# Small marker loads behind the big loads of a fused attention-plus-GLU decode kernel

## The chip, the cores and the metric

The kernel runs on one core of one Trainium2 chip. The metric is device time in microseconds (us). The profile is one profiled execution; its span, from the first to the last instruction that the profile shows, is a little shorter than the device time, which also holds what lies around it.

## What is computed

One decode step for two batch rows: a layer norm of x, then attention with 32 heads over the last 2048 positions of the caches, and beside it a gated linear unit without a nonlinearity. All is float32.

```python
xn = _layernorm(x)
q = (xn @ wq)                                     # 2 rows, 32 heads of 128
scores = einsum("bhqd,bhkd->bhqk", q, k[..., -2048:, :]) * 128 ** -0.5
a = einsum("bhqk,bhkd->bhqd", softmax(scores), v[..., -2048:, :]) @ wo
h = (xn @ w_gate) * (xn @ w_up)                   # 1376 wide
return x + a + h @ w_down
```

Nearly all bytes are the caches: K and V of 32 heads for two rows. Every byte is used once.

## The kernel before

The host lays out all weights and caches in one long array, `stream`, in the order in which the kernel uses them. `blocks()` (L45) gives that order as a list of loads; each load is a list of fields (a head's K, 4096 floats wide in each of 128 partitions, a head's V, a slice of a weight). The first load goes to a tile of its own, `first`, 542 floats wide. All others go to step tiles: `steps` (L128) is a pool with three buffers of 128 partitions by STEP = 13824 floats (L39), that is 55296 bytes in each partition. Most loads fill a step tile; those at the end of the stream are smaller, and several share a tile.

`pump()` (L143) issues loads from SP until three step tiles are held; `done()` (L166) counts a field as used up, and when the last field of a tile is used, it frees the tile and calls `pump()` again, so that the next load is issued then. The load into a freed buffer waits on SP until VectorE and TensorE have finished with the buffer. All loads go out on SP's DMA queue, in order. Two small DMAs stand behind the fourth load on the same queue: `x_nat` (L182), 16 rows of 128 floats, and `carry` (L185), 9 rows of 9 floats. The result goes out at L531.

For each head VectorE multiplies K with the projected query in place (`products`, L277) and sums over the head dimension (`sums`, L285); GpSimd and ScalarE make the softmax; TensorE weighs V, and projects queries, outputs and the gated unit. One such step over a head's K occupies VectorE for two instructions over 4096 floats.

`InOrder` (L83) keeps each engine's instructions in the order in which the program lists them, and records all of them under one line, L98; in the profile, operations are told apart by their tiles. SP executes in order as well: an instruction that waits holds back all behind it.

Tiles of the pool `const` (L127) lie one behind the other in each partition in the order in which they are made, and the step tiles lie behind them. A DMA counts as landed when a semaphore says so; the small tile's dependencies are tracked tile by tile, so that two DMAs that write the same tile are ordered by a wait.

Of the kernel before, what the change touches and what calls it, by code (L numbers as in the profile page):

```python
# [8 lines left out]
F32 = mybir.dt.float32  # L9
# [18 lines left out]
RB = 8  # L28
M = RB * (B - 1) + 1
# [84 lines left out]
def kernel(  # L114
# [8 lines left out]
    pe, dve, act, sp = (InOrder(tc, e) for e in (nc.tensor, nc.vector, nc.scalar, nc.sync))  # L123
# [3 lines left out]
    const = ctx.enter_context(tc.tile_pool(name="const", bufs=1))  # L127
# [8 lines left out]
        todo.append((key, fields, at))  # L136
        at += P * sum(w for _, _, w in fields)
    tiles, used, left, got = {}, {}, {}, {}
    held = 0
    for key, fields, _ in todo:  # L140
        left[key] = left.get(key, 0) + len(fields)

    def pump():  # L143
        nonlocal held
        while todo:
            key, fields, at = todo[0]
            if key not in tiles:
                if key[0] == "f":
                    n = sum(w for _, _, w in fields)
                    tiles[key] = const.tile([P, n], F32, name="first")  # L150
                elif held == BUFS:
                    return
                else:
                    held += 1
                    tiles[key] = steps.tile([P, STEP], F32, name="step")
                used[key] = 0
            todo.pop(0)
            c0 = used[key]
            for kind, i, w in fields:
                got[kind, i] = (tiles[key][:, used[key] : used[key] + w], key)  # L160
                used[key] += w
            c1 = used[key]
            src = stream[at : at + P * (c1 - c0)].rearrange("(p i) -> p i", p=P)
            sp.dma_start(tiles[key][:, c0:c1], src)

    def done(kind, i):  # L166
        nonlocal held
        _, key = got.pop((kind, i))
        left[key] -= 1
        if left[key] == 0 and key[0] != "f":  # L170
            del tiles[key]
            held -= 1
            pump()

    pump()
    xT = got["x", 0][0].rearrange("p (b c) -> p b c", b=B)
    pick = got["pick", 0][0].rearrange("p (r s b) -> p r s b", s=2, b=B)
# [447 lines left out]
```

## Time and profile before

| What | Value |
|---|---|
| Time, median of 3 runs | 377.29 us (377.18 to 377.37) |
| Profiled execution, span | 375.7 us |
| Read from HBM in that span | 159.47 MB |
| Mean DMA rate over the span | 425 GB/s |
| Matmuls, TensorE | 1100 |
| Loads into step tiles | 28 |

How to read the profile: PE is TensorE (PEld its weight loads), DVE VectorE, ACT ScalarE, POOL GpSimd, SP the engine whose queue issues the DMAs; SPq, DVEq are the engines' instruction queues. Rows of grouped instructions read: line, engine, operation, written tile <- read tiles, count. DMA rows give the size of one in KB (1024 bytes) and the time from its issue to its landing. "DMA share" is the mean busy share of the 16 DMA engines; a packet is counted where it starts, so that a short stretch can exceed 1. A queue row reads: packets, MB, and the time that the packets took as a share of 16 engines' time.

### The profile page before, as it was taken

The numbers are of one execution on the slowest core, as the hardware profiler recorded it, in microseconds if no ns is written. First come the engines' busy times: TensorE is split into PE (matmuls) and PEld (weight loads), VectorE is DVE, ScalarE is ACT, GpSimd is POOL, SyncE is SP. The second block draws the span as 40 slices with busy tenths as digits, with TensorE's granted clock in tenths as the row PEclk, the third lists the DMA queues.
The fourth block names the chain that finished last, engine by engine and source line by source line (L and its number), as shares of the span: only waits on it lengthen the run. The fifth ranks groups of instructions, "written<-read, shape, count | busy, mean of one in ns | idle before, by whom it ended". The sixth has DMA issues, their size and how long they took to land.

```text
span 375.7 us, 2891 instructions
## 1 busy us (share of the span) xinstructions
PE 256.5 (68%) x1100; PEld 88.1 (23%) x1100; DVE 294.6 (78%) x147; ACT 58.7 (16%) x259; POOL 25.3 (7%) x78
## 2 busy tenths in 40 slices
PE   3396696986548487864848676485867639637996
PEld 3241122331112122211222211121212213021334
DVE  3299691998599499769949976994996799599960
ACT  1021001122020211201112020111202011121131
POOL 1001000000000000100000100000000000000010
PEclk9796988899696966859686786976669887556999
DMA  8999999899999999999999999999999999999995
GB/s 327 463 436 454 408 426 471 383 465 432 414 465 394 459 424 424 461 400 453 418 437 449 412 447 424 432 442 430 436 436 424 437 434 436 436 425 424 419 421 226
DMA packets 4382, 159.70 MB, mean 425 GB/s; under 512 B 514, under 2 KB 658, under 8 KB 1042
## 3 DMA queue, kind: packets, MB, share of 16 engines
q1 hardware_dynamic: 4370, 159.54, 98.5%
q8 instruction: 8, 0.13, 0.1%
q14 instruction: 4, 0.03, 0.0%
HBM read 159.47 MB, written 0.07 MB: 425 GB/s over the span
## 4 chain that ended last, share of the span: by engine, by line
DMA 62%; DVE 29%; PE 7%; ACT 1%; issue 0%; SPq 0%; DVEq 0%
DMA step<-in_stream_dram 62%; DVE s L98 14%; DVE step L98 14%; PE o_ps L98 3%; PE q L98 2%; PE acc L98 2%; PE tr L98 1%; DVE m L98 0%; ACT o_sb L98 0%; ACT oT L98 0%; SPq L98 0%; DVE rec L98 0%; DVE o_out L98 0%; DVEq L98 0%
## 5 line engine op out<-in xcount | busy, mean ns | idle before, releaser
L98 DVE TENSOR_TENSOR step<-step,q 128x4096 f32<-128x4096 f32 x31 | 136.6, 4408 | 53.3 <-DMA step<-in_stream_dram 53.3
L98 PE MATMUL q<-step,xnb 128*128 128x512 f32 (+1 forms) x128 | 92.7, 874 | 75.5 <-DMA step<-in_stream_dram 75.5
L98 DVE TENSOR_REDUCE s<-step 128x32 f32<-128x4096 f32 x32 | 141.4, 4419 | 1.1
L98 PE MATMUL o_ps<-step,p 128*16 128x512 f32 (+1 forms) x512 | 69.7, 682 | 10.3 <-DMA step<-in_stream_dram 10.3
L98 PEld LDWEIGHTS q<-step,xnb 128*128 128x128 f32 x128 | 32.2, 275 | 128.9 <-DMA step<-in_stream_dram 79.1
L98 PE MATMUL acc<-step,oT 128*9 128x512 f32 (+1 forms) x88 | 35.2, 554 | 9.3 <-ACT oT L98 8.1
L98 PE MATMUL tr<-first,o_sb 128*128 128x2 f32 (+2 forms) x198 | 27.6, 258 | 15.3 <-ACT o_sb L98 12.8
L98 ACT COPY o_sb<-o_ps 128x512 f32<-128x512 f32 (+1 forms) x24 | 13.8, 576 | 143.1 <-PE o_ps L98 143.1
L98 PEld LDWEIGHTS tr<-first,o_sb 128*128 128x128 f32 x198 | 25.5, 196 | 37.3 <-ACT o_sb L98 32.6
L295 POOL PARTITION_ALL_REDUCE mm<-m x32 | 11.3, 354 | 283.4 <-DVE rec L98 178.9
L98 PEld LDWEIGHTS o_ps<-step,p 128*16 128x16 f32 x512 | 13.5, 106 | 70.4 <-issue 55.2
L98 ACT ACTIVATE nm<-mm 128x2 f32<-128x2 f32 x32 | 6.5, 203 | 129.5 <-POOL mm L295 129.5
L98 ACT ACTIVATE p<-s,nm 128x16 f32<-128x16 f32 x64 | 19.2, 300 | 1.0
L98 ACT ACTIVATE oT<-tr,rec 128x1 f32<-128x1 f32 x64 | 12.2, 260 | 28.3 <-PE tr L98 28.3
L311 POOL PARTITION_ALL_REDUCE sum<-rs x32 | 12.7, 398 | 54.8 <-ACT p L98 54.8
L98 PE MATMUL o_ps<-step,xn 128*2 128x512 f32 (+1 forms) x48 | 12.9, 593 | 0.0
L98 ACT ACTIVATION_READ_ACCUMULATOR p<-s,nm 128x1 f32 x64 | 12.0, 187 | 0.0
L98 DVE TENSOR_TENSOR step<-step,tr 128x4096 f32<-128x4096 f32 x1 | 4.4, 4421 | 9.3 <-DMA step<-in_stream_dram 9.3
L98 PEld LDWEIGHTS acc<-step,oT 128*9 128x9 f32 x88 | 4.3, 91 | 19.5 <-ACT oT L98 13.1
L98 PE MATMUL q<-xnb,mean_w 128*128 128x512 f32 (+1 forms) x18 | 8.5, 563 | 0.0
L98 PE MATMUL acc<-step,hT 128*9 128x128 f32 (+2 forms) x58 | 7.9, 357 | 0.0
L98 DVE TENSOR_REDUCE m<-s 128x2 f32<-128x32 f32 x32 | 5.9, 186 | 1.1
(43 smaller groups left out, 36.5 us busy)
## 6 DMA issues: line engine op xcount, KB each, us to landing
step<-in_stream_dram SPq DMA_DIRECT2D x16, 6912.0 KB, 33.7
step<-in_stream_dram SPq DMA_DIRECT2D x2, 6400.0 KB, 32.6
step<-in_stream_dram SPq DMA_DIRECT2D x1, 6720.0 KB, 45.6
step<-in_stream_dram SPq DMA_DIRECT2D x1, 6656.0 KB, 28.9
step<-in_stream_dram SPq DMA_DIRECT2D x1, 5376.0 KB, 15.4
step<-in_stream_dram SPq DMA_DIRECT2D x1, 4864.0 KB, 30.1
step<-in_stream_dram SPq DMA_DIRECT2D x2, 2304.0 KB, 17.2
step<-in_stream_dram SPq DMA_DIRECT2D x1, 2048.0 KB, 15.9
```

The lines of the kernel that those rows point to most:

```text
L98: made = call(*args, **kwargs)
L295: nc.gpsimd.partition_all_reduce(mm, m, P, bass_isa.ReduceOp.max)
L311: nc.gpsimd.partition_all_reduce(sum_t[h], rs, P, bass_isa.ReduceOp.add)
```

## The change

A tile `marks`, 16 partitions of 40 floats (160 bytes in each partition), is made before all others of `const`. `pump()` counts its loads. Behind the sixth to the twentieth load, counted with `first` as number one, it issues one more DMA on SP: k = 1 for the sixth, up to 15 for the twentieth; k rows of 8 + 2k floats each, from the array `x_rows` into `marks`. The fourteenth load (k = 9 = M) has none. Nothing reads `marks`. The computing instructions of the other engines and their order stay the same.

```diff
-    held = 0
+    held = n_loads = 0
+    marks = const.tile([2 * RB, 5 * RB], F32, name="marks")
...
     def pump():
-        nonlocal held
+        nonlocal held, n_loads
...
             sp.dma_start(tiles[key][:, c0:c1], src)
+            n_loads += 1
+            k = n_loads - 5
+            if 0 < k < 2 * RB and k != M:
+                sp.dma_start(marks[:k, : 8 + 2 * k], x_rows[:k, : 8 + 2 * k])
```

## The prediction

> **What bounds the kernel now.** I read the page from the top (busy shares, the DMA line, the chain of waits), then the 50-us windows, then the rows of SP's queue. In the page below, DMA is busy nearly the whole span and the chain that ended last is mostly one kind of wait, a load of the stream:
>
> ```profile
> span 375.7 us, 2891 instructions
> PE 256.5 (68%) x1100; PEld 88.1 (23%) x1100; DVE 294.6 (78%) x147; ACT 58.7 (16%) x259; POOL 25.3 (7%) x78
> ...
> q1 hardware_dynamic: 4370, 159.54, 98.5%
> ...
> DMA 62%; DVE 29%; PE 7%; ACT 1%; issue 0%; SPq 0%; DVEq 0%
> ```
>
> The reader is to see that no engine is near its limit (VectorE, the busiest, has 22% idle) while SP's DMA queue, q1, fills 98.5% of the 16 DMA engines' time. The VectorE pieces of the chain are not a bound of their own: they are the time until a buffer is free, and meanwhile earlier loads still stream, as a window from the middle shows (last two columns: DMA share, GB/s):
>
> ```profile
> 200.00:250.00 50.00, 33.96 (x128) 10.58 (x124) 44.38 (x21) 7.77 (x36) 3.76 (x10) 0.75 1.01 435
> ```
>
> So the time is bytes over about 435 GB/s plus start and end. Anything added to this queue counts in full only if it takes DMA-engine time, or delays an issue until the queue runs dry. I priced both.
>
> **What the change adds.** One tile of 160 bytes per partition, and 14 small DMAs on SP: k from 1 to 15 without 9, k rows each, one behind each big load concerned; k rows because the sum 1+...+15 less 9 is 111 rows. Nothing is removed, and the order of the computing engines' work is the same. The built program shows one wait more: each small DMA writes the tile that the one before wrote, so SP holds it until that one has landed, and the next big load stands behind it.
>
> *DMA-engine time.* The kernel already has such a DMA: `carry`, 9 rows of 36 bytes, behind `x_nat`, 16 rows of 512 bytes, behind a 6720 KB load. Windows on the DMA packets, each on a stretch so short that it holds one packet or a few, give the time of a packet as share x 16 engines x stretch:
>
> ```profile
> DMA packets 1, 0.00 MB, mean 18 GB/s; under 512 B 1, under 2 KB 1, under 8 KB 1
> q1 hardware_dynamic: 1, 0.00, 34.4%
> ...
> DMA packets 1, 0.00 MB, mean 0 GB/s; under 512 B 1, under 2 KB 1, under 8 KB 1
> q1 hardware_dynamic: 1, 0.00, 5.6%
> ...
> q1 hardware_dynamic: 7, 0.00, 12.6%
> ```
>
> The first stretch is 2 ns (46.740 to 46.742 us) and holds one `carry` row: 0.344 x 16 x 2 = 11 ns. The second is 10 ns and holds one semaphore write of 4 bytes: 0.056 x 16 x 10 = 9 ns. The third is 50 ns where x_nat and carry pass: 7 packets in 0.126 x 16 x 50 = 101 ns, 14 ns each. A row of the small loads has 40 to 152 bytes, between carry's 36 and x_nat's 512, so 14 ns is a fair price, and 14 + 9 = 23 ns for row and semaphore. If k rows go to k engines, the busiest engine serves all 14: 14 x 23 = 0.32 us; the mean engine 111 / 16 x 23 ns = 0.16 us. The last load waits for the slowest engine, so between 0 (that engine has slack) and 0.32 us; I take 0.2. The upper bound is by landings:
>
> ```profile
> step<-in_stream_dram SPq DMA_DIRECT2D x1, 6720.0 KB, 45.6
> x_nat<-in_x_rows_dram SPq DMA_DIRECT2D x1, 8.0 KB, 45.3
> ...
> 1.15 1.37 SPq L98 DMA_DIRECT2D step<-in_stream_dram  x3
> 2.56 0.55 SPq L98 DMA_DIRECT2D x_nat<-in_x_rows_dram  x1
> ...
> out_dram<-o_out SPq DMA_DIRECT2D x1, 64.0 KB, 1.5
> ```
>
> The third big load was issued about 2.1 us into the span (three in 1.37 us) and landed at 47.7; x_nat at 2.56 + 45.3 = 47.9. Were this 0.2 us time in which nothing else moved, 14 of them would be 2.8 us: the far end. It should not be, since a completion can trail while the next packets run.
>
> [...]
>
> *The held issues.* SP's rows and the landings of the same loads, each issue looked at by itself:
>
> ```profile
> 73.14 0.33 SPq L98 DMA_DIRECT2D step<-in_stream_dram  x1
> step<-in_stream_dram SPq DMA_DIRECT2D x1, 6912.0 KB, 24.7
> ...
> 83.19 0.33 SPq L98 DMA_DIRECT2D step<-in_stream_dram  x1
> step<-in_stream_dram SPq DMA_DIRECT2D x1, 6912.0 KB, 31.0
> ...
> 92.26 0.33 SPq L98 DMA_DIRECT2D step<-in_stream_dram  x1
> step<-in_stream_dram SPq DMA_DIRECT2D x1, 6912.0 KB, 38.3
> ...
> 126.47 0.33 SPq L98 DMA_DIRECT2D step<-in_stream_dram  x1
> step<-in_stream_dram SPq DMA_DIRECT2D x1, 6912.0 KB, 36.6
> ```
>
> These loads land at 97.8, 114.2, 130.6 and 163.1, so one takes 16.3 us. The small DMA issued behind the load of 83.19 waits for the small one behind the load of 73.14, which lies in the queue behind that load: 97.8 and a little. The load of 92.26 stands behind it on SP and is held to about 99 (6 us late). Its data follow on those of the load landing at 114.2, so it is still 15 us early. The same recurs at every second load, the one issued more than one load ahead now: the load of 126.47 is held until the one landing at 130.6 has landed, 5 us, and 15 us remain. The loads between are issued after that point anyway. Behind the held load on SP there is only its own small DMA; no engine waits for SP itself, and VectorE and TensorE wait for landings, which do not move. Price: 0. Without this cover it would be 5 or 6 us at some six loads, about 33 us. The small DMA's own issue, some 0.55 us as for x_nat, is hidden in the same 15 us.
>
> *The shift by 160 bytes.* The small tile is allocated first, so every later tile moves. In the built program the three step tiles begin at multiples of 2048 bytes in their partition, afterwards 32 bytes past a multiple of 64. What a row there costs no trace of before shows; the nearest rows are the `first` load, 2168-byte rows to a tile that begins 128 bytes past a multiple of 256, from a source whose rows lie 2168 bytes apart, against 2048-byte rows of the last load, well placed:
>
> ```profile
> q1 hardware_dynamic: 78, 0.17, 72.2%
> ...
> q1 hardware_dynamic: 1, 0.00, 52.5%
> ...
> L98 SPq DMA_DIRECT2D step<-in_stream_dram x28: 327/328/432, 1.1 to 353.5; - x28
> ```
>
> The first stretch is 0.6 us: 0.722 x 16 x 600 / 78 = 89 ns a row; the second 10 ns: 84 ns. The 120 bytes between them take 4.4 ns at 435 / 16 = 27.2 bytes/ns, so bad placement costs 0.5 ns a row. The 28 step loads give 28 x 128 / 16 = 224 rows to each engine: 0.1 us, the value I take. The far end: all that a 2168-byte row takes above its bytes, 89 - 80 = 9 ns, paid once more by each row, 224 x 9 = 2.0 us. Below nothing: a worse placement cannot gain. The Trainium skill, "DMA: Bandwidth & Descriptors", section How a descriptor splits into AXI transactions, says that a descriptor off a multiple of 256 bytes starts at the border below it and spends beats on bytes it doesn't need; it says so of reads. If writes did likewise, a shifted row would pay 8 beats of 32 bytes more at most, by the page's 850 MHz an estimate of 9 ns, and the sum would be 2 us higher. This trace's 0.5 ns speaks against it.
>
> **Sum**, against this execution: span 375.7 + 0.2 + 0 + 0.1 = 376.0. The median of the runs, 377.29, lies 1.59 above this span, which I leave as it is: 376.0 + 1.6 = 377.6 us. A change within 0.2% (0.75 us) is here no change.
>
> **The rivals.**
>
> *Small DMAs in series* (slower): the queue stands still until a small DMA has completed. For it: the extra wait on completion, and nothing shows a small DMA between two full loads in the steady part. Against: the 101 ns in which packets of three DMAs pass. Price: 0.2 us x 14 = 2.8, so 380.1; at the worst the 1.5 us that the lone output DMA takes, 14 x 1.5 = 21 us, 398. It decides from 0.06 us per small DMA (0.75 / 14). Chance 0.13. [...]
>
> *Misplaced rows* (slower): the shifted tiles make each packet longer. Price up to 2.0 us, 379.5 with the small DMAs' 0.2; decides from 3 ns a row (0.75 us / 224). Against: the 0.5 ns. For: the placement of before was exact, and 32 bytes past 64 is not what the 89 ns row has. Chance 0.17; a twentieth of all chance is in it for a far larger price, which I can't bound.
>
> *All rows on one engine* (the spreading does not happen): one engine serves 111 rows and 14 semaphore writes, 111 x 14 + 14 x 9 = 1.7 us, 379.0 if that engine is the last to finish. For it: nothing but that the built program does not say which engines a DMA uses. Against: x_nat and carry packets pass one behind the other on several engines within the 50 ns above (101 ns of packets in 50 ns are three engines at least). Chance 0.04.
>
> *Instruction fetches* (either way). These take the same 16 engines, on a queue of their own:
>
> ```profile
> q8 instruction: 8, 0.13, 0.1%
> ```
>
> 0.1% of 16 x 375.7 us over 8 fetches is about 0.75 us for one engine each (0.4 to 1.1, since the share is rounded). One more fetch for SP's longer program, on the engine that ends last: about 378.4, chance 0.03. Or the fetches fall on other engines than before, the slowest engine is spared one, and the loads, all issued in time, end 0.75 to 1.1 us sooner: 376.5 to 376.9. That is the only gain I find, since no work goes away and the queue is at 435 GB/s already. Chance 0.08.
>
> **How the numbers follow.** The forecast, everything hidden but 0.1 to 0.4 us, has 0.55, and its own range is 377.2 to 377.9; with it goes the part of the misplaced rows that stays under 0.75 us, 0.05. Within 0.2%: 0.60. Slower: 0.13 in series, 0.12 misplaced, 0.04 one engine, 0.03 fetch: 0.32. Faster: 0.08. The range reaches down to 376.9, into the faster case, and up to 380.2, over the misplaced rows' 379.5 and the 380.1 of the series; outside are the far ends, 0.05 of the misplaced rows, about 0.04 of the series and about half of the faster case, 0.13 together.
>
> **What would show it.** Right: 222 packets more, nearly all under 512 bytes (111 rows and 111 semaphore writes, a few more if the single row is split); loads issued near 99 and 131 us that stood at 92.26 and 126.47 before, with their landings still 16.3 us apart; steady windows at 435 GB/s; SP with new waits on DMA, VectorE and TensorE with none. Wrong, by place: landings further apart by 0.2 us or more only behind the small loads (series); packets of 55296 bytes longer than in the stretch from 200 to 250 us of before, all over the span (placement); a single engine behind the others (no spreading); DMA share falling to some tenths before a held load (the cover was too small). That stretch of before has 441 packets, 48 of them of 4 bytes:
>
> ```profile
> DMA packets 442, 21.75 MB, mean 435 GB/s; under 512 B 48, under 2 KB 48, under 8 KB 48
> q1 hardware_dynamic: 441, 21.73, 100.4%
> ```
>
> 1.004 x 16 x 50 us less 48 x 9 ns, over 393 rows, is 2043 ns a row.

## The result, and the profile after

| | before | after |
|---|---|---|
| Median of 5 runs | 377.29 us | 378.79 us |
| Lowest to highest | 377.18 to 377.37 | 378.73 to 378.95 |
| Span of the profiled execution | 375.7 us | 377.0 us |

The changed kernel is 1.50 us slower; the ratio is 1.004, with a 95% interval of 1.0027 to 1.0053. That is outside the 0.2% within which the forecast had it most likely, and inside the range.

The page of the changed kernel:

```profile
span 377.0 us, 2904 instructions
PE 256.7 (68%) x1100; PEld 89.1 (24%) x1100; DVE 294.6 (78%) x147; ACT 58.6 (16%) x259; POOL 25.5 (7%) x78
...
q1 hardware_dynamic: 4592, 159.55, 98.3%
...
DMA 83%; DVE 14%; PE 1%; SPq 0%; issue 0%; DVEq 0%
DMA marks<-in_x_rows_dram 66%; DMA step<-in_stream_dram 16%; DVE s L98 7%; DVE step L98 7%; PE acc L98 0%; SPq L98 0%; PE tr L98 0%; PE o_ps L98 0%; PE q L98 0%; DVE m L98 0%; DVE o_out L98 0%; DVE rec L98 0%; DVEq L98 0%
```

VectorE's busy time is that of before to the tenth of a microsecond, and q1 has 222 packets more, as worked out. The chain looks alarming: 66% of the span now runs through `marks`. It misleads here. SP now goes from one small DMA's landing to the next, so the chain follows them back; but a small DMA lies in the queue behind a big load, and nearly all of its time is that load's. How SP's queue goes, by rows of the timeline (start, length, what):

```profile
73.02 0.33 SPq L98 DMA_DIRECT2D step<-in_stream_dram  x1
79.88 0.26 SPq L98 DMA_DIRECT2D marks<-in_x_rows_dram  x1
83.52 0.33 SPq L98 DMA_DIRECT2D step<-in_stream_dram  x1
96.44 0.27 SPq L98 DMA_DIRECT2D marks<-in_x_rows_dram  x1
96.89 0.33 SPq L98 DMA_DIRECT2D step<-in_stream_dram  x1
113.50 0.27 SPq L98 DMA_DIRECT2D marks<-in_x_rows_dram  x1
116.29 0.33 SPq L98 DMA_DIRECT2D step<-in_stream_dram  x1
130.26 0.28 SPq L98 DMA_DIRECT2D marks<-in_x_rows_dram  x1
130.65 0.33 SPq L98 DMA_DIRECT2D step<-in_stream_dram  x1
```

The loads of 92.26 and 126.47 are issued at 96.89 and 130.65, right behind a small DMA that was held; those between go out when they did. So the hold is there, and the question is whether it, the small packets, or the shift costs the 1.50 us.

The last VectorE instruction, the output's sum, divides the span into the stream with its tail, and the end behind it. Before and after:

```profile
373.02 0.29 DVE L98 TENSOR_TENSOR o_out<-acc,x_nat 128x128 f32<-128x128 f32 x1 [8.16 <-PE acc L98]
```

```profile
373.86 0.29 DVE L98 TENSOR_TENSOR o_out<-acc,x_nat 128x128 f32<-128x128 f32 x1 [8.13 <-PE acc L98]
```

The stream ends 0.84 us later. From there to the end of the span it takes 377.0 - 373.86 = 3.1 us, against 375.7 - 373.02 = 2.7: another 0.45 us behind everything that the stream does. Two places, then, and the experiments take them apart. Together they make 1.3 of the 1.50 us. The other 0.2 us lie in the execution that was profiled before: its span is 375.7 us, while the kernel before, timed again beside the experiments, has a median span of 375.5 to 375.6.

### The profile page after: what moved, and what is told of

The parts are those of the page before. It is cut to its first block, busy times and chain, and to the rows that moved or that the text cites. A ratio compares the mean times of both kernels' runs of the same rounds, so it can differ in the third digit from the quotient of the medians.

```text
span 377.0 us, 2904 instructions
## 1 busy us (share of the span) xinstructions
PE 256.7 (68%) x1100; PEld 89.1 (24%) x1100; DVE 294.6 (78%) x147; ACT 58.6 (16%) x259; POOL 25.5 (7%) x78
## 4 chain that ended last, share of the span: by engine, by line
DMA 83%; DVE 14%; PE 1%; SPq 0%; issue 0%; DVEq 0%
DMA marks<-in_x_rows_dram 66%; DMA step<-in_stream_dram 16%; DVE s L98 7%; DVE step L98 7%; PE acc L98 0%; SPq L98 0%; PE tr L98 0%; PE o_ps L98 0%; PE q L98 0%; DVE m L98 0%; DVE o_out L98 0%; DVE rec L98 0%; DVEq L98 0%
## 5 line engine op out<-in xcount | busy, mean ns | idle before, releaser
L98 PE MATMUL q<-step,xnb 128*128 128x512 f32 (+1 forms) x128 | 94.7, 892 | 74.6 <-DMA step<-in_stream_dram 74.6
L98 PE MATMUL acc<-step,oT 128*9 128x512 f32 (+1 forms) x88 | 34.2, 543 | 9.3 <-ACT oT L98 8.1
L98 DVE RECIPROCAL rec<-sum 128x2 f32<-128x2 f32 x32 | 5.0, 155 | 2.2 <-POOL sum L316 2.2
```

What stands on the lines that cost most here:

```text
L98: made = call(*args, **kwargs)
```

## The experiments

Each was timed beside the kernel before on the same chip, whose median was 377.27 to 377.38. The lines of a profile are of one execution, which lies up to 0.5 us off the median of its kernel. "Steps in place" means that the step tiles begin at multiples of 2048 bytes, as before.

### The tile alone, and the small DMAs alone

The tile without any small DMA (`e1_tile_only`):

```diff
-                sp.dma_start(marks[:k, : 8 + 2 * k], x_rows[:k, : 8 + 2 * k])
+                pass
```

> The tile of 160 bytes alone, no small DMA: all tiles lie where the changed kernel has them. Against the kernel before, the changed one is 1.5 us slower; its profile has the output sum starting 0.84 us later (373.86 against 373.02), 0.46 us more after the output's landing, and rows of 55296 bytes of about 2044.6 ns instead of 2041.4. Theory A (placement makes the rows longer): rows near 2044.6 here, output sum 0.5 to 0.6 us late, 377.8 to 377.9. Theory B (the small DMAs make the rows behind them longer) and theory C (the held issues do): rows at 2041.4, 377.3. Theory D (SP's longer program costs the 0.46 us at the end): none of it here, under A, B or C.

The small DMAs with the steps in place (`e2_marks_in_place`):

```diff
-    marks = const.tile([2 * RB, 5 * RB], F32, name="marks")
+    marks = const.tile([2 * RB, 4 * P], F32, name="marks")
```

> The change with the small tile made 2048 bytes wide in its partitions, so that the step tiles begin at multiples of 2048 bytes as before. Theory A: rows back at 2041.4 ns, leaving the small packets (0.2 to 0.3 us) and the end (0.46 us): 378.0 to 378.2. Theories B and C: rows stay at 2044.6, 378.8. Theory D: the 0.46 us at the end stay.

Measured: the tile alone 378.14, ratio 1.0022 (1.0013 to 1.0031); the small DMAs alone 377.80, ratio 1.0014 (1.0005 to 1.0023). That is 0.87 and 0.53 over the 377.27 beside them, 1.40 together of the 1.50. The output's sum starts, tile alone and small DMAs alone:

```profile
core 0 of [0], span 376.5 us
...
373.81 0.29 DVE L98 TENSOR_TENSOR o_out<-acc,x_nat 128x128 f32<-128x128 f32 x1 [8.27 <-PE acc L98]
```

```profile
core 0 of [0], span 376.2 us
...
373.01 0.29 DVE L98 TENSOR_TENSOR o_out<-acc,x_nat 128x128 f32<-128x128 f32 x1 [7.69 <-PE acc L98]
```

A clean cut. A tile that nothing writes makes the stream 0.79 us longer and leaves the end at 376.5 - 373.81 = 2.7; the 14 small DMAs leave the stream where it was and make the end 3.2. DMA packets that start between 256 and 290 us show how the stream is stretched. Before, the tile alone, the small DMAs alone:

```profile
DMA packets 300, 14.82 MB, mean 436 GB/s; under 512 B 32, under 2 KB 32, under 8 KB 32
q1 hardware_dynamic: 300, 14.82, 100.6%
```

```profile
DMA packets 301, 14.87 MB, mean 437 GB/s; under 512 B 32, under 2 KB 32, under 8 KB 32
q1 hardware_dynamic: 301, 14.87, 101.2%
```

```profile
DMA packets 351, 14.88 MB, mean 438 GB/s; under 512 B 82, under 2 KB 82, under 8 KB 82
q1 hardware_dynamic: 351, 14.88, 101.1%
```

All but the small ones are rows of 55296 bytes. Share x 16 x 34 us, less 9 ns for each of 32 semaphore writes (some 11 ns for each of the 82 small packets of the last), over the rows: 2041 ns before, 2045.5 with the tile alone, 2041 with the small DMAs alone, each good to about 1 ns. The same stretch in the changed kernel has 349 packets, 82 of them small, at a share of 100.6%: 2046 ns. Three to five nanoseconds a row, and some 190 rows of all lengths on each engine from 70 us on, give 0.6 to 0.9 us: an estimate, which fits the 0.79.

### Which tiles, and which multiple

The whole change, its tile of 160 bytes too, with the padding of `carry` cut by as much, so that the steps are in place while the tiles ahead of them stay shifted (`e5_steps_in_place`):

```diff
-CARRY = 72
+CARRY = 72 - 5 * RB
```

> The whole change with its tile of 160 bytes, and the padding of the carry tile cut by 160 bytes: the step tiles begin at multiples of 2048 bytes as before, all tiles ahead of carry's end are shifted as in the changed kernel. Theory A1 (the place of the step tiles makes the rows of the stream longer): rows of 2041.4 ns, output sum at 373.0, 377.8 as with the wide tile. Rival A2 (the shift of the other tiles does it, by the engines' own accesses to them): rows of 2044.5, output sum at 373.8, 378.8.

Measured: 377.79, ratio 1.0014 (1.0005 to 1.0022), output's sum at 372.71. Its packets between 256 and 290 us read as those of the small DMAs alone. So it is the place of the step tiles, and one line gives back 1.0 of the 1.5 us with everything else of the change kept.

Tiles of 128 and of 256 bytes, nothing written to them (`e6_tile_128`, `e7_tile_256`):

```diff
-    marks = const.tile([2 * RB, 5 * RB], F32, name="marks")
+    marks = const.tile([2 * RB, 4 * RB], F32, name="marks")
...
-                sp.dma_start(marks[:k, : 8 + 2 * k], x_rows[:k, : 8 + 2 * k])
+                pass
```

(8 * RB for 256 bytes.)

> No small DMA; a tile of 128 bytes alone, so that the step tiles begin 128 bytes past a multiple of 256. The tile of 160 bytes alone gave rows of 2044.2 ns and 378.14 (0.87 over before). Theory A1a (what counts is a multiple of 64 bytes): rows 2041.4, 377.3. Theory A1b (a row is written in pieces that end at multiples of 256): rows near 2044, 378.1.

> No small DMA; a tile of 256 bytes alone, step tiles at a multiple of 256 and not of 512. Theories A1a and A1b: rows 2041.4, 377.3. Rival A1c (512 bytes or more count): rows near 2044, 378.1.

Measured: 128 bytes 378.16, ratio 1.0023 (1.0014 to 1.0032), output's sum at 373.65; 256 bytes 377.33, ratio 1.0000 (0.9992 to 1.0009), output's sum at 372.83. The packets between 256 and 290 us with 128 and with 256 bytes:

```profile
q1 hardware_dynamic: 301, 14.87, 101.2%
```

```profile
q1 hardware_dynamic: 302, 14.93, 101.4%
```

With 32 small ones each that is 2045.5 and 2042 ns a row. A shift of 128 costs as much as one of 160, one of 256 nothing: the border is a multiple of 256 bytes. It isn't the 64 bytes of theory A1a.

### Rows in a small load, and the hold

All 16 rows in each small load (`e3_all_16_rows`), and columns of its own for each, so that none waits for the one before (`e4_no_hold`), both with the steps in place:

```diff
-                sp.dma_start(marks[:k, : 8 + 2 * k], x_rows[:k, : 8 + 2 * k])
+                sp.dma_start(marks[:, : 8 + 2 * k], x_rows[:, : 8 + 2 * k])
```

```diff
-                sp.dma_start(marks[:k, : 8 + 2 * k], x_rows[:k, : 8 + 2 * k])
+                c = (k - 1) * (8 + k)
+                sp.dma_start(marks[:k, c : c + 8 + 2 * k], x_rows[:k, : 8 + 2 * k])
```

> As the run before with the wide tile, and each small load takes all 16 rows, so that all engines serve all 14. Theory B in the form that loads on some engines alone put the engines out of step: rows back at 2041.4 ns, 378.1 (packets 0.3, end 0.46). Theory B in the form that any small DMA does it: rows at 2044.6 or more, 378.8 to 379.0. Theory A: 378.1 as in the run with the wide tile alone. Theory C: 378.8.

> Wide tile, and each small load writes columns of its own, so that none waits for the one before and the big loads are issued when they were before (92.3 and 126.5 us again instead of 96.9 and 130.7). Theory C: rows back at 2041.4 ns, and 0.5 us less than with the hold. Theory B: rows at 2044.6, no change from the run with the hold. Theory D: SP has fewer instructions that wait; if that takes its program back over the border, the 0.46 us at the end are gone: 378.3, otherwise they stay.

Measured: 377.91, ratio 1.0016 (1.0007 to 1.0025), and 377.58, ratio 1.0008 (0.9999 to 1.0016). How many rows a small load has makes no difference to be told from the 377.80 with k rows. With columns of its own a small DMA doesn't wait, although it writes the same tile: the wait goes by the part of the tile that is written, not by the whole tile as the part on the kernel before has it. Without the hold SP's queue is that of before again:

```profile
92.24 0.33 SPq L98 DMA_DIRECT2D step<-in_stream_dram  x1
92.61 0.33 SPq L98 DMA_DIRECT2D marks<-in_x_rows_dram  x1
115.66 0.33 SPq L98 DMA_DIRECT2D step<-in_stream_dram  x1
116.04 0.34 SPq L98 DMA_DIRECT2D marks<-in_x_rows_dram  x1
126.39 0.33 SPq L98 DMA_DIRECT2D step<-in_stream_dram  x1
```

The loads go out at 92.24 and 126.39, and the output's sum of that execution starts at 373.37, not earlier than the 373.01 with the hold. That execution is among the slowest of its eleven (378.04 us, median 377.58), so its stream says little by itself; the medians differ by 0.2 us. The end takes 376.2 - 373.37 = 2.8 us instead of 3.2, and that alone is more than the 0.2 us. So no cost of the hold to the stream is to be seen.

### The end, and the price of a small DMA

Seven small DMAs (even k), three (k = 2, 4, 6), and 56 (four behind each load, in columns of their own), all with the steps in place:

```diff
-            if 0 < k < 2 * RB and k != M:
+            if 0 < k < 2 * RB and k % 2 == 0:
```

```diff
-            if 0 < k < 2 * RB and k != M:
+            if k in (2, 4, 6):
```

```diff
-    marks = const.tile([2 * RB, 5 * RB], F32, name="marks")
+    marks = const.tile([2 * RB, 12 * P], F32, name="marks")
...
-                sp.dma_start(marks[:k, : 8 + 2 * k], x_rows[:k, : 8 + 2 * k])
+                for n in range(4):
+                    c = 3 * P * n + (k - 1) * (8 + k)
+                    sp.dma_start(marks[:k, c : c + 8 + 2 * k], x_rows[:k, : 8 + 2 * k])
```

> Wide tile, step tiles at multiples of 2048, and only the small DMAs of even k: 7 instead of 14. With 14 in place the stream ended when it did before (output sum at 373.02 against 373.02) and the 0.53 us were all behind the output's landing: 1.29 us from there to the end of the span against 0.83 before. Theory D (SP's program, longer by its DMAs and waits, crosses a border where the next piece must be fetched, near the end of the program): a step, 0.83 or 1.3 us, by where the border falls; 377.3 if it isn't reached, 377.8 if it is. Rival D2 (each small DMA costs the end its share, say by more semaphores to settle): half of it, 1.06 us, 377.55.

> Step tiles at multiples of 2048, small loads for k = 2, 4 and 6 alone. With 14, one more fetch of program code (8192 bytes) showed at 376.5 us, within the span, and the end took 1.29 us from the output's landing; with 7 it showed at 377.4 us, behind the span, the end took 0.90 us and the time outside the span grew by 0.3 us; in the kernels without small DMAs there is none. Theory D (SP's program crosses a border): with three the border lies behind the program, no such fetch, 377.3. Rival D2 (a share for each small DMA, 0.53 / 14): 377.4, no step. If the fetch is still there and the time is 377.7, the border is nearer than I take it.

> Step tiles at multiples of 2048, and four small loads of the same shape in columns of their own behind each big load concerned: 56 instead of 14. Theory P (a small DMA takes the time of its row and its semaphore write on the engines it uses, 23 ns, and nothing else): 56 x 23 ns = 1.3 us on the engine that serves all, 0.6 us on the mean one; output sum between 373.0 and 374.3, 378.0 to 379.1 with the 0.5 us of the end. Rival S (each holds the queue for 0.06 us or more until it has completed): 56 x 0.06 to 0.2 = 3.4 to 11 us, 381 or more. Rows of 2041.4 ns in both.

One thing in the second of these was put wrongly: the fetch with 14 small DMAs, at 376.5 us, lies 0.3 us behind its span's end of 376.2, not within it.

| small DMAs | median, us | ratio, interval | output's sum at | from there to span's end | extra fetch at |
|---|---|---|---|---|---|
| 0 (before) | 377.29 | | 373.02 | 2.7 | none |
| 3 | 377.57 | 1.0006 (0.9997 to 1.0015) | 372.81 | 3.0 | none |
| 7 | 377.70 | 1.0011 (1.0002 to 1.0020) | 372.75 | 2.7 | 377.4 |
| 14 | 377.80 | 1.0014 (1.0005 to 1.0023) | 373.01 | 3.2 | 376.5 |
| 14, no hold | 377.58 | 1.0008 (0.9999 to 1.0016) | 373.37 | 2.8 | 375.6 |
| 56 | 377.97 | 1.0019 (1.0010 to 1.0028) | 373.56 | 2.7 | 251 |

The last column is a fetch of program code that the kernel before does not have. It shows on queue q14. With 14 small DMAs, between 374 and 380 us, and with 56, between 248 and 256 us, where the kernel before has one:

```profile
q14 instruction: 1, 0.01, 0.4%
```

```profile
q14 instruction: 2, 0.02, 0.5%
```

What SP does at the end (the program's last line; count, then shortest, median and longest in ns), before, after, with 56, and with 14 without the hold, this one with q14 between 374 and 376.2 us, the end of its span:

```profile
L620 SPq DRAIN  x3: 7/7/7, 375.0 to 375.3; - x3
...
SPq L620 <- DMA out_dram<-o_out: 0.9, 1, 0.9
```

```profile
L625 SPq DRAIN  x3: 7/7/114, 376.0 to 376.7; - x3
...
SPq L625 <- DMA out_dram<-o_out: 1.1, 1, 1.1
```

```profile
L627 SPq DRAIN  x3: 7/7/7, 375.5 to 375.8; - x3
...
SPq L627 <- DMA out_dram<-o_out: 0.9, 1, 0.9
```

```profile
L626 SPq DRAIN  x3: 7/7/7, 375.5 to 375.8; - x3
...
q14 instruction: 1, 0.01, 0.9%
```

The delay stands at SP's last drain: from the first to the last of the three it takes 0.7 us in the changed kernel and 0.3 in the others, and one of them is 114 ns long instead of 7. A drain of over 100 ns stands in four traces, those in which 14 small DMAs wait for one another (the changed kernel, the small DMAs alone, the steps in place, all 16 rows), and in no other. So it is no share for each small DMA: with 56 it isn't there, and with 14 that don't wait for one another it isn't either.

That the extra fetch causes it is not shown. In these four traces the fetch starts only behind the end of the span, when the drain is over: between 374 and 377 us the changed kernel has no packet on q14. And without the hold the fetch falls among SP's last instructions, at 375.6 us, and the drains take 0.3 us as before. With 56 it lies in the middle of the kernel, where SP is waiting anyway. Fetch and long drain both come with more instructions on SP; what the drain waits for stays open.

With seven the fetch falls behind the span. The spans of those runs have a median of 375.6 us, against 375.5 for the kernel before beside them, while the time is 0.38 above: 0.3 us of it lie outside the span, and what they are the profile doesn't show.

The other part of the end, 0.2 us of 1.1 against 0.9, is the order of the last waits: in the changed kernel SP meets its wait for the output earlier in the row, so that it settles other DMA semaphores after the output has landed. With three small DMAs there is no fetch and no long drain, and the wait for the output is 1.2 us: 0.3 us, all at the end of that execution, though the medians can't tell three from none. Theory D as put, a step of 0.46 or nothing, fits the long drain, not its cause, and left this part out.

The stream itself: with the steps in place and 3 to 14 small DMAs that wait for one another the output's sum starts at 372.7 to 373.0, with 56 at 373.56, 0.5 to 0.9 us later. Over 42 to 53 more, that is 0.01 to 0.02 us each, in the size of the 23 ns that their packets take on an engine. The rival of 0.06 us or more each would have shown 3.4.

## Why the prediction was right and wrong

- **What bounds the kernel**: right. What the shift costs the stream is time of DMA packets; VectorE's busy time stayed at 294.6.
- **DMA-engine time of the small loads**: right in size. 222 packets more; 0.2 us was taken for 14, the runs put them between nothing and 0.3, and 56 at 0.5 to 0.9.
- **The held issues**: right. Forecast about 99 and 131, found 96.89 and 130.65; price 0, and no cost to the stream is to be seen when the hold is taken away.
- **The shift**: the mechanism was named, as the rival of the misplaced rows with a chance of 0.17, and the term in the sum was mis-sized. It was taken as 0.1 us, 0.5 ns for each of 224 rows; it measured 3 to 5 ns a row from about 70 us on and 0.87 us by itself, in the middle of the 0 to 2.0 us that the bounds left. What failed is the step from a row of `first`, 2168 bytes long and written while the kernel starts, to rows of 55296 bytes in the stream. Both the length and the stage matter. Rows of 18432 bytes, between 351.5 and 360.5 us, before and with the tile alone:

```profile
q1 hardware_dynamic: 230, 3.83, 99.2%
```

```profile
q1 hardware_dynamic: 232, 3.82, 99.3%
```

  Less the 22 and 25 semaphore writes among them, that is 686 and 690 ns a row: about as much more as a row three times as long pays. Rows of 2048 bytes of the last load, before (371.4 to 371.8 us) and with the tile alone (372.1 to 372.5 us):

```profile
q1 hardware_dynamic: 39, 0.07, 46.5%
```

```profile
q1 hardware_dynamic: 32, 0.05, 32.8%
```

  Less 4 and 8 semaphore writes, that is 84.0 and 84.5 ns: so short a row pays the 0.5 ns of the forecast even there. And early in the kernel a long row pays nothing. Packets between 33 and 43 us, before and with the tile alone:

```profile
q1 hardware_dynamic: 83, 4.46, 103.1%
```

```profile
q1 hardware_dynamic: 83, 4.46, 103.0%
```

  All 83 are rows of 53760 bytes: 1.031 x 160 us / 83 = 1987 ns and 1986. The Trainium skill, "DMA: Bandwidth & Descriptors", section How a descriptor splits into AXI transactions, had the border right: 256 bytes, although it speaks of reads; its beats made at most 9 ns a row, the trace has 3 to 5. It was set aside on the word of a short row from another stage.
- **The end**: missed. The sum had the time behind the stream unchanged; it is 0.45 us longer, 0.2 by the order of SP's last waits and the rest at its last drain. A longer program on SP was among the rivals, as a fetch that takes 0.75 us of a DMA engine in the stream. The fetch came, but behind the stream, and no run shows that it is what holds the drain. The Trainium skill, "Runtime: NRT & Kernel Launch", section Instruction fetch mechanics, says that the cost of crossing into the next block of a program is mostly hidden; with the fetch at 251 us and at 375.6 us the traces agree.
- **In series, one engine**: fell. 56 small DMAs cost 0.6 us in all, and 16 rows in place of k cost no more. One reading there was too strong: 101 ns of packets in 50 ns show two engines at least, not three, since a packet counts with its whole length where it starts.

So 377.6 was 1.2 us short: about 0.75 for the shift, 0.45 for the end. That the range held the time is in part luck: its upper end was set by small DMAs in series, which did not come, and the end was in none of its terms.

## What to carry to other kernels

In a kernel that a DMA stream bounds, a tile is not free because nothing reads it: look where the large tiles behind it come to lie, and keep their starts at multiples of 256 bytes; 160 bytes ahead of them cost more here than 14 DMAs. Price such a thing by rows of the length and from the stage that the sum is about: a row of 2 KB showed 0.5 ns of it and a long row early in the kernel none. And look behind the last landing as well: DMAs added to a queue that has time to spare all through the kernel can still be met at its end.

## What was not expected of the hardware

- Rows at 128 or 160 bytes past a multiple of 256 take 2045 to 2046 ns instead of 2041 in the steady stream, and no more than well placed ones between 33 and 43 us. What differs between the stages was not found: the same tiles are written in both. Rows of 18432 bytes pay about as many nanoseconds as these, rows of 2048 bytes 0.5.
- A DMA of 40 to 152 bytes a row between two loads of 6912 KB takes 0.01 to 0.02 us of the stream, although SP sees it land some 16 us after its issue, about when the load ahead of it lands.
- SP's last drain takes over 100 ns instead of 7 in the four traces in which 14 small DMAs wait for one another; the cause is open.
- The fetch on q14 is of 8192 bytes. That it is SP's code is inferred from its place, which moves with what is added on SP alone; the trace doesn't name the engine.
